# A sorted block attention with a gated feed-forward layer: a new order of the opening stage (value chunks behind key chunks, a four-fold mixing matrix, first weight loads behind the keys)

## The chip, the cores and the metric

The kernel runs on one core of one Trainium2 chip. The metric is the device time of one execution in microseconds (us), as the median of the runs. Names used: PE is TensorE (matmuls), PEld its weight loads, DVE is VectorE, ACT is ScalarE, POOL is GpSimd, SP is SyncE. SBUF is the working memory, PSUM the memory of eight banks into which PE writes; a bank has 512 float32 columns.

## The reference

```python
# q, k, v: (4 batches, 8 heads, 768 rows, 64); sort_net: (4, 8, 8, 8)
P = sort_net
for _ in range(5):                       # Sinkhorn: rows, then columns
    P = exp(P - max(P, -1)); P /= sum(P, -1) + 1e-9; P /= sum(P, -2) + 1e-9
# 8 blocks of 96 rows; each block of keys and values becomes a mix of all 8
k_sorted = einsum('bhij,bhjcd->bhicd', P, k_blocks)
v_sorted = einsum('bhij,bhjcd->bhicd', P, v_blocks)
attn = softmax(q_block @ k_sorted_block.T / sqrt(64))       # 96 x 96, per block
x = (attn @ v_sorted_block)  -> (3072 tokens, 512)
g = x @ w_gate               # 512 x 1536
out = (g * sigmoid(g) * (x @ w_val)) @ w_out                # 1536 x 512
```

All inputs and the output are float32; the kernel computes in bfloat16 with float32 sums.

## The kernel before

**Stages.** The 3072 tokens are eight groups of 384 (a half of the blocks of one batch, `n` = 0 to 7). For each group the attention gives `xts[(b, half)]`, four slices of 128 rows by 384 tokens; then `ffn(n)` makes 12 gate groups and 12 value groups of four matmuls each (`gate` L381, `value` L399), and three output tiles in three parts (`outp` L413), which run in the list of the next group. `merge` (L569) puts a list of side tasks (mixing of later batches' keys and values, scores, attention) between the gate and value groups, each task behind the point where the summed cost of the main list (0.65 for a gate or value group, 0.87 for a part of an output tile) reaches its due time. The order on PE and POOL is the program's. On DVE and ACT it is the program's up to L537 as well; from there on it is planned at compile time.

**The mixing.** The five Sinkhorn rounds work on `p_ps` (32 x 64, L193 to L211). Their result goes as `p_bf` (L186, L212 to L216) into `weights` (L461), where PE transposes it for every block i into `w_ps`: one matmul spreads one block over 64 partitions, eight copies of the 8 values of j, and `weights` runs once for the lower and once for the upper half. `mix_rows` (L467) multiplies `w_ps` by a 0/1 mask, which gives the block-diagonal mixing matrix `rmix` of a batch; that of batch 0 is made at once, those of batches 1 to 3 later (L490).

**The first 25 us** prepare batch 0 without any other work to lie beside. Its queue order is written out by hand:

- POOL issues all casting loads: v of batch 0 in two halves (L144, L145), half of q, k in two halves (L149), then copies its share of v into `vch` (`copy_v`, L150 to L152: each partition's 96 x 64 values turned round, so that one column is one d over all 96 rows c), then issues the first 256 columns of both weight matrices (`load_gv`, L153), the rest of q, three more `load_gv`, v of batch 1, the last two `load_gv`, and k, q of batch 1 and the output weights. At most eight such loads are under way; the ninth issue waits for the landing of the first.
- ACT copies the other share of v (L201, L203, L217, L218).
- PE keeps busy with small matmuls and fillers (`dots`, `fill`, L444 to L457), makes `w_ps`, and then chunks: `q0_chunk` (L249), `v_chunk` (L268) and `k0_chunk` (L258) each mix or transpose some columns into a PSUM tile, and DVE ("v") or ACT ("s") drains it to `kqt` or `vt`. The last argument is the PSUM tag: "a" and "b" are pairs of banks, "x" is one bank, "gen" is a set of three single banks, of which `w_ps` holds one until the last `mix_rows` has read it. A chunk waits for the drain of the one before it in its bank.
- `qk` (L323) makes the scores of one pair of heads over four blocks and their exponentials on ACT (`exps`); `av` (L326) multiplies them with `vt`, whose row carries 64 values and a one (so the 65th column is the sum), and DVE divides (`r_sb` L338, `st` L340). `x_to` transposes `st` into x, `drain` copies it, and `early` (L514) starts the first gate and value groups.

**Values of batch 1** are turned by POOL once they have landed (L595) and mixed by `v_chunk` inside `merge(ffn(1), ...)` (L608), followed by the keys and queries (`kqs`) and the first attention units of batch 1.

Of the kernel before, what the change touches and what calls it, by code (L numbers as in the profile page):

```python
# [10 lines left out]
BF16 = mybir.dt.bfloat16  # L11
AF = mybir.ActivationFunctionType
ALU = mybir.AluOpType
# [4 lines left out]
def kernel(  # L18
# [11 lines left out]
    nc = tc.nc  # L30

    B, H, S, D = q.shape
# [80 lines left out]
    def load_gv(lo, hi):  # L113
        load_w(wg_sb, wg_dram, lo, hi)
        load_w(wv_sb, wv_dram, lo, hi)

    def copy_v(eng, pair, rows, s, n=4, d0=0, d1=D):
        cs = slice(s * (C // n), (s + 1) * (C // n))
        dst = vch3[rows, d0:d1, cs]
        src = v_tiles[pair][rows, cs, d0:d1]  # L120
        if eng is nc.scalar:
            eng.copy(dst, src.transpose([0, 2, 1]))  # L122
        else:
            eng.tensor_copy(dst, src.transpose([0, 2, 1]))  # L124
# [22 lines left out]
    load_q0(0)  # L147
    for a, rows in enumerate(halves):
        nc.gpsimd.dma_start(out=k0[rows], in_=k_nat[0, :, a * HC:(a + 1) * HC, :])  # L149
    copy_v(nc.gpsimd, 0, lowr, 0)  # L150
    copy_v(nc.gpsimd, 0, lowr, 3)
    copy_v(nc.gpsimd, 0, lowr, 5, 8, 40, D)  # L152
    load_gv(0, 256)  # L153
    load_q0(1)
    for m in range(256, 1024, 256):
        load_gv(m, m + 256)
    load_v(1, 0, C)
    for m in range(1024, DF, 256):
        load_gv(m, m + 256)
    load_k(1, 0, C)  # L160
    load_q(1, 0, C)
    nc.gpsimd.dma_start(out=wo_sb, in_=wo_dram)
# [6 lines left out]

    def vt_tile(pair):  # L170
        if pair not in vts:
            t = vtp.tile([C, 2, H * NB, D + 4], BF16, name=f"vt{pair}", tag="vt")
            nc.vector.memset(t[:, :, :, D:D + 1].rearrange("p u n e -> p (u n) e"), 1.0)
            vts[pair] = t
        return vts[pair]
# [7 lines left out]

    rowreds = [const.tile([BH, NB, 1], FP32, name=f"rowred{it}") for it in range(N_ITER)]
    colred = const.tile([BH, 1, NB], FP32)
    p_bf = const.tile([BH, NB, H, NB], BF16)  # L186
    def pair_tile(name, tag):
        return psum.tile([128, 1024], FP32, name=name, tag=tag)

    def bank_tile(name, tag="gen"):  # L190
        return psum.tile([128, 512], FP32, name=name, tag=tag, bufs=3 if tag == "gen" else 1)

    p_ps = bank_tile("p_ps")[0:BH, 0:NB * NB].rearrange("p (i j) -> p i j", j=NB)  # L193
    for it in range(N_ITER):
# [14 lines left out]
        nc.vector.reciprocal(colred, colred)  # L209
        if it < N_ITER - 1:  # L210
            nc.vector.tensor_mul(p_ps, p_ps, colred.to_broadcast([BH, NB, NB]))  # L211
    for lo in (0, NB // 2):  # L212
        part = slice(lo, lo + NB // 2)
        nc.vector.tensor_tensor(
            p_bf[:, part], p_ps[:, part].unsqueeze(2).to_broadcast([BH, NB // 2, H, NB]),
            colred.unsqueeze(1).to_broadcast([BH, NB // 2, H, NB]), op=ALU.mult)  # L216
    copy_v(nc.scalar, 0, lowr, 4, 8)  # L217
    copy_v(nc.scalar, 0, lowr, 5, 8, 0, 40)  # L218

# [29 lines left out]
    def q0_chunk(t, at, n, eng, tag):  # L249
        dst = kqt_tile(0)[:, GI * C:2 * GI * C].rearrange("p (g t r c) -> p t g r c", g=H2, t=2, c=QC)[:, t]  # L250
        tp = chunk_tile("tq0", n // 8, tag).rearrange("p (l g r) -> p l g r", l=n, g=H2)
        for lc in range(n):
            for two in range(2):
                nc.tensor.matmul(tp[two * D:(two + 1) * D, lc], lhsT=q0[t][:, at + lc, :],
                                 rhs=sel[:, two], start=True, stop=True)
        drain(eng, dst[:, :, :, at:at + n], tp.rearrange("p l g r -> p g r l"))

    def k0_chunk(at, n, eng, tag):  # L258
        dst = kqt_tile(0)[:, 0:GI * C].rearrange("p (n a c) -> p a n c", a=2, c=HC)
        rm = rmix[0].rearrange("p a (g two) i -> p two a g i", two=2)  # L260
        tp = chunk_tile("tk0", n // 8, tag).rearrange("p (l a n) -> p l a n", l=n, a=2)
        for lc in range(n):
            for two in range(2):
                nc.tensor.matmul(tp[two * D:(two + 1) * D, lc].rearrange("p a (g i) -> p a g i", g=H2),
                                 lhsT=k0[:, at + lc, :], rhs=rm[:, two], start=True, stop=True)
        drain(eng, dst[:, :, :, at:at + n], tp.rearrange("p l a n -> p a n l"))

    def v_chunk(b, at, n, eng, tag):  # L268
        rows = slice(0, 128) if b % 2 else lowr
        dst = vt_tile(b // 2)[:, b % 2]  # L270
        mix = rmix[b][rows, 0].rearrange("p a b -> p (a b)")
        tp = chunk_tile("tv", n // 8, tag).rearrange("p (l n) -> p l n", n=H * NB)
        for ld in range(n):
            col = (at + ld) * C
            nc.tensor.matmul(tp[:, ld, :], lhsT=vch[rows, col:col + 128], rhs=mix,  # L275
                             start=True, stop=True)
        drain(eng, dst[:, :, at:at + n], tp[0:C].transpose([0, 2, 1]))
# [45 lines left out]
    def qk(b, u, tag="b"):  # L323
        exps(b, u, *scores(b, u, tag))

    def av(b, u, tag="a"):  # L326
        half, g = divmod(u, H2)
        vt = vts[b // 2][:, b % 2].rearrange("p (h i) e -> p h i e", h=H)
        av_ps = pair_tile("av_ps", tag).rearrange("p (two n) -> p two n", two=2)
        o = av_ps.rearrange("p two (i e) -> p two i e", i=4)  # L330
        for two in range(2):
            e = es[(b, u)][two]
            for i4 in range(4):
                nc.tensor.matmul(o[:, two, i4, 0:D + 1], lhsT=e[:, i4 * C:i4 * C + 128],  # L334
                                 rhs=vt[:, 2 * g + two, half * 4 + i4, 0:D + 1],
                                 start=True, stop=True)
        r_sb = ssp.tile([C, 2, 4, 1], FP32, name="r_sb", tag="r")
        nc.vector.reciprocal(r_sb, o[0:C, :, :, D:D + 1])  # L338
        st = ssp.tile([C, 4, 2, D], BF16, name="st", tag="st")
        nc.vector.tensor_tensor(st.rearrange("p i two d -> p two i d"), o[0:C, :, :, 0:D],  # L340
                                r_sb.to_broadcast([C, 2, 4, D]), op=ALU.mult)
        sts[(b, u)] = st
# [101 lines left out]
    def fill(tile, n):  # L444
        for _ in range(n):
            nc.tensor.matmul(tile, lhsT=warm_sb[:, 0:128], rhs=warm_sb, start=True, stop=True)  # L446
# [9 lines left out]
                         start=True, stop=True)  # L456
        fill(idle_ps, n)  # L457

    w_ps = bank_tile("w_ps")[:, 0:NB * B * H].rearrange("p (i b h) -> p i b h", b=B, h=H)

    def weights(half):  # L461
        for i in range(NB):
            nc.tensor.matmul(w_ps[halves[half], i].rearrange("p b h -> p (b h)"),
                             lhsT=p_bf[:, i].rearrange("p a b -> p (a b)"),
                             rhs=ident[0:BH, 0:BH], start=True, stop=True)

# [1 line left out]
        nc.vector.tensor_tensor(dst, mask[rows].unsqueeze(2).to_broadcast([R, H, NB]),  # L468
                                w_ps[rows, :, b].transpose([0, 2, 1]), op=ALU.mult)

    weights(0)
    weights(1)
    mix_rows(rmix[0][lowr, 0], lowr, 0)
    mix_rows(rmix[0][highr, 1], highr, 0)
    q0_chunk(0, 0, 16, "s", "b")
    v_chunk(0, 0, 8, "v", "gen")
    v_chunk(0, 8, 8, "s", "gen")
    v_chunk(0, 16, 16, "v", "a")
    v_chunk(0, 32, 8, "v", "gen")
    v_chunk(0, 40, 16, "s", "b")  # L480
    v_chunk(0, 56, 8, "s", "gen")
    k0_chunk(0, 16, "v", "a")
    k0_chunk(16, 16, "s", "b")
    k0_chunk(32, 8, "v", "gen")
    k0_chunk(40, 8, "s", "gen")
    q0_chunk(0, 16, 8, "v", "a")
    fill(idle_ps, 4)
    qk(0, 0, "a")
    qk(0, 1, "b")
    for b in range(1, B):  # L490
        rows = halves[b % 2]
        mix_rows(rmix["p"][rows, b % 2] if b > 1 else rmix[1][rows, 0], rows, b)
    qk(0, 2, "gen")
    idle_ps = bank_tile("idle_ps")
    fill(idle_ps, 2)
    av(0, 0, "a")
    fill(idle_ps, 2)
    av(0, 1, "b")
    fill(idle_ps, 1)
    xts[(0, 0)] = xtp.tile([128, H2, TW], BF16, name="xt0_0", tag="xt")  # L500
    qk(0, 3, "gen")
    av(0, 2, "a")
# [1 line left out]
    x_to(x01[:, 0], 0, 0)  # L504
    x_to(x01[:, 1], 0, 1)
    drain("s", xts[(0, 0)][:, 0:2, :], x01.rearrange("p g a b -> p g (a b)"))
    fill(idle_ps, 1)
    av(0, 3, "b")
    x2 = xt_tile("gen", 1)
    x_to(x2[:, 0], 0, 2)  # L510
# [47 lines left out]
    def kqs(b, ats):  # L558
        return [(at, lambda n=n: (kq_chunk(b, n * 32, 16, "v", "b"), kq_chunk(b, n * 32 + 16, 16, "s", "a")))
                for n, at in enumerate(ats)]  # L560

    def vs(f, size, ats):
        return [(at, lambda m=m: f(1, m * size, size, "sv"[m % 2], "ba"[m % 2])) for m, at in enumerate(ats)]
# [5 lines left out]
    def merge(main, side):  # L569
        done, k = 0.0, 0  # L570
        side = sorted(side, key=lambda t: t[0])
        for c, f in main:
            f()
            done += c
            while k < len(side) and side[k][0] <= done:
                side[k][1]()
                k += 1
        while k < len(side):
            side[k][1]()
            k += 1  # L580
# [22 lines left out]
    def q0_rest():  # L603
# [1 line left out]
        q0_chunk(1, 16, 8, "v", "a")  # L605

    merge(ffn(0), [(0.0, q0_rest)] + units(0, range(4, 8), (2.0, 6.6)))
    merge(ffn(1), vs(v_chunk, 16, (3.2, 3.9, 4.7, 5.5)) + kqs(1, (6.2, 8.2, 10.3))  # L608
          + units(1, range(4), (11.3, 16.4), (3.1, 2.5)))
    for s in range(4):  # L610
        copy_v(nc.gpsimd, 1, both, s)
# [43 lines left out]
```

## Time and profile before

| what | us |
|---|---|
| median of 3 runs | 248.45 (248.39 to 252.37) |
| the profiled execution | 249.62 |
| its span, first to last instruction | 247.7 |
| PE busy | 239.4 (97%) |
| PEld busy | 140.7 (57%) |
| DVE busy | 157.1 (63%) |
| ACT busy | 109.5 (44%) |
| POOL busy | 51.9 (21%) |
| granted TensorE clock | 1.000 |

Times of single events below are those of the profiled execution, counted from the start of its span. A busy engine is not an engine that sets the end: matmuls overlap, and PE's fillers count as busy. A line of the chain of work that ended last is a start, a length, and the engine with what it writes and the line of the code. In other rows the bracket gives the idle time of the engine just before, and what ended it.

### The profile page before, as it was taken

The page shows a single profiled execution, that of the slowest core. Times are in us where ns is not written, and L with a number is a line of the kernel's source. Part 1 is how long each engine was busy: PE and PEld are TensorE (multiplying, and loading weights), DVE is VectorE, ACT ScalarE, POOL GpSimd, SP SyncE. Part 2 cuts the span into 40 slices and gives each one's busy share as a digit, 9 for nine tenths or more (in the row PEclk, how much of TensorE's full clock was granted, in tenths as well). Part 3 has the DMA queues.
Part 4 walks back from the last instruction along what each step waited for, and adds up shares of the span by engine and source line. Part 5 has one row for each costly group of instructions (what it writes and reads, how often), then busy time and mean ns, then how long its engine had stood idle before and what let it go on. Part 6 is the DMA issues. An engine that isn't in the chain of part 4 may idle for free.

```text
span 247.7 us, 6185 instructions
## 1 busy us (share of the span) xinstructions
PE 239.4 (97%) x2633; PEld 140.7 (57%) x2633; DVE 157.1 (63%) x332; ACT 109.5 (44%) x186; POOL 51.9 (21%) x45
## 2 busy tenths in 40 slices
PE   8799998999999999999999999999999999999995
PEld 6375665666555556655555655565555555555543
DVE  6686789787556775857657646755764585446700
ACT  3877652453544444444642552354245334232311
POOL 5993459960049300000000000000000000000000
PEclk9999999999999999999999999999999999999999
DMA  5999999999999287010122121112111121100122
GB/s 98 214 120 181 218 191 219 194 227 215 215 164 179 41 201 173 4 42 3 45 56 52 55 62 34 44 42 78 32 42 45 39 57 54 42 21 25 42 81 88
DMA packets 39578, 24.38 MB, mean 98 GB/s; under 512 B 27712, under 2 KB 35648, under 8 KB 39104
## 3 DMA queue, kind: packets, MB, share of 16 engines
q0 software_dynamic: 21376, 14.16, 39.3%
q1 hardware_dynamic: 18176, 9.84, 13.9%
q8 instruction: 20, 0.33, 0.5%
q14 instruction: 6, 0.05, 0.1%
HBM read 28.32 MB, written 7.86 MB: 146 GB/s over the span
## 4 chain that ended last, share of the span: by engine, by line
PE 83%; DVE 9%; ACT 2%; issue 2%; DMA 2%; DVEq 0%; POOLq 0%
PE v_ps L403 23%; PE o_ps L420 23%; PE g_ps L385 22%; PE tkq L244 3%; PE av_ps L334 2%; PE qk L307 2%; DVE st L340 2%; DMA v<-in_v_dram 2%; DVE gs_sb L395 2%; DVE h L408 2%; DVE vt L222 1%; PE o_ps L436 1%; PE idle_ps L446 1%; PE tv L275 1%; ACT th_sb L393 1%
## 5 line engine op out<-in xcount | busy, mean ns | idle before, releaser
L395 DVE SCALAR_TENSOR_TENSOR gs_sb<-th_sb,g_ps 128x384 bf16<-128x384 bf16 x96 | 52.8, 550 | 51.5 <-ACT th_sb L393 48.7
L403 PE MATMUL v_ps<-xt,wv_sb 128*128 128x384 bf16 x380 | 77.3, 326 | 1.1 <-DVE st L340 0.7
L385 PE MATMUL g_ps<-xt,wg_sb 128*128 128x384 bf16 x376 | 76.7, 326 | 0.1
L393 ACT ACTIVATE th_sb<-g_ps 128x384 bf16<-128x384 f32 x96 | 47.1, 490 | 57.0 <-PE g_ps L385 54.5
L420 PE MATMUL o_ps<-wo_sb,h 128*128 128x512 bf16 x276 | 64.0, 379 | 0.0
L408 DVE SCALAR_TENSOR_TENSOR h<-v_ps,gs_sb 128x384 bf16<-128x384 f32 x96 | 53.3, 555 | 6.9
L403 PEld LDWEIGHTS <-wv_sb 128*128 128x128 bf16 x380 | 35.1, 97 | 24.9 <-issue 1.9
L385 PEld LDWEIGHTS <-wg_sb 128*128 128x128 bf16 x376 | 34.7, 97 | 23.5 <-issue 0.4
L420 PEld LDWEIGHTS <-h 128*128 128x128 bf16 x276 | 26.3, 98 | 28.9
L425 ACT COPY o_sb<-o_ps 128x512 f32<-128x512 f32 x23 | 13.5, 585 | 50.9 <-PE o_ps L420 50.9
L124 POOL COPY vch<-v 64x1536 bf16<-64x1536 bf16 (+2 forms) x11 | 28.6, 2635 | 21.1 <-DMA v<-in_v_dram 21.0
L320 ACT ACTIVATE e_all<-qk 96x768 bf16<-96x768 f32 x30 | 22.6, 802 | 7.6 <-PE qk L307 7.6
L340 DVE TENSOR_TENSOR st<-av_ps,r_sb 96x512 bf16<-96x512 f32 x32 | 21.7, 679 | 0.2
L334 PEld LDWEIGHTS <-e_all 96*128 96x128 bf16 x256 | 12.0, 97 | 4.9 <-ACT e_all L320 0.9
L334 PE MATMUL av_ps<-vt,e_all 96*128 96x65 bf16 x256 | 13.2, 193 | 0.0
L222 DVE CAST vt<-tv 96x1024 bf16<-96x1024 f32 (+1 forms) x9 | 9.8, 1096 | 2.6 <-PE tv L285 1.6
L338 DVE RECIPROCAL r_sb<-av_ps 96x8 f32<-96x8 f32 x32 | 6.4, 199 | 8.0 <-PE av_ps L334 7.9
L224 ACT CAST vt<-tv 96x1024 bf16<-96x1024 f32 (+1 forms) x9 | 8.1, 913 | 3.0 <-PE tv L285 1.8
L446 PE MATMUL idle_ps<-warm_sb 128*128 128x512 bf16 x25 | 7.7, 416 | 0.0
L222 DVE COPY oh_sb<-o_ps 128x256 f32<-128x256 f32 x1 | 0.4, 423 | 9.3 <-PE o_ps L436 9.3
L122 ACT COPY vch<-v 64x768 bf16<-64x768 bf16 (+1 forms) x4 | 5.4, 1375 | 0.7 <-DMA v<-in_v_dram 0.7
L370 POOL DMA_DIRECT2D q_scr<-in_q_dram x2 | 5.7, 3228 | 0.0
(80 smaller groups left out, 135.3 us busy)
## 6 DMA issues: line engine op xcount, KB each, us to landing
out_dram<-o_sb SPq DMA_DIRECT2D x23, 256.0 KB, 2.0
v<-in_v_dram POOLq DMA_DIRECT2D x3, 768.0 KB, 19.9
wg_sb<-in_moe_w_gate_dram POOLq DMA_DIRECT2D x6, 256.0 KB, 11.1
wv_sb<-in_moe_w_val_dram POOLq DMA_DIRECT2D x6, 256.0 KB, 11.9
wo_sb<-in_moe_w_out_dram POOLq DMA_DIRECT2D x1, 1536.0 KB, 23.8
kp<-in_k_dram POOLq DMA_DIRECT2D x2, 768.0 KB, 15.1
q_scr<-in_q_dram POOLq DMA_DIRECT2D x2, 768.0 KB, 29.9
v<-in_v_dram POOLq DMA_DIRECT2D x2, 384.0 KB, 6.4
```

Source lines behind the costliest of these rows:

```text
L124: eng.tensor_copy(dst, src.transpose([0, 2, 1]))
L222: nc.vector.tensor_copy(dst, src)
L320: nc.scalar.activation(e_all[:, n:n + 2, 0:4 * C], wide[0:C, :, 0:4 * C], AF.Exp, scale=scale)
L334: nc.tensor.matmul(o[:, two, i4, 0:D + 1], lhsT=e[:, i4 * C:i4 * C + 128], rhs=vt[:, 2 * g + two, half * 4 + i4, 0:D + 1], start=True, sto ...
L340: nc.vector.tensor_tensor(st.rearrange("p i two d -> p two i d"), o[0:C, :, :, 0:D], r_sb.to_broadcast([C, 2, 4, D]), op=ALU.mult)
L385: nc.tensor.matmul(g_ps, lhsT=wg_sb[:, kc, ts(m, 128)], rhs=xt[:, kc, :], start=(kc == 0), stop=(kc == NKC - 1))
L393: nc.scalar.activation(th_sb, g_ps, AF.Tanh, scale=0.5)
L395: nc.vector.scalar_tensor_tensor(gs_sb, th_sb, 1.0, g_ps, op0=ALU.add, op1=ALU.mult)
L403: nc.tensor.matmul(v_ps, lhsT=wv_sb[:, kc, ts(m, 128)], rhs=xt[:, kc, :], start=(kc == 0), stop=(kc == NKC - 1))
L408: nc.vector.scalar_tensor_tensor(h_tiles[n][:, m, :], v_ps, 0.5, gs_tiles.pop(m), op0=ALU.mult, op1=ALU.mult)
L420: nc.tensor.matmul(o_ps, lhsT=h_w[:, m, ts(t3, 128)], rhs=wo_sb[:, m, :], start=(m == 0), stop=(m == NFC - 1))
L425: nc.scalar.copy(o_sb, o_ps)
```

## The change

It reorders the first 25 us and two later places:

1. The first weight load (256 columns of both matrices) is issued behind k and ahead of POOL's copies of v.
2. The weight loads up to column 1280 go ahead of v of batch 1 (before: up to 1024).
3. A row of `vt` is 72 elements wide, not 68 (65 are used).
4. `p_bf` holds four copies of a block's row, not eight, written by one DVE instruction instead of two; `w_ps` is made by 32 matmuls over 32 partitions each instead of 16 over 64.
5. The chunks of batch 0 are cut and ordered anew: q's second chunk comes before the third value chunk, the last 16 of the 64 value columns come behind the keys, the keys are cut into 8, 8, 8, 16, 8, and the bank "x" is used for three chunks.
6. The four fillers ahead of the scores are half as wide and write into the unused half of the bank of `w_ps` (`fill_w`); the third scores come ahead of the mixing matrices of batches 1 to 3; there are fewer fillers behind.
7. The value chunks of batch 1 get later due times, and its key and query chunks too.

```diff
     for a, rows in enumerate(halves):
         nc.gpsimd.dma_start(out=k0[rows], in_=k_nat[0, :, a * HC:(a + 1) * HC, :])
+    load_gv(0, 256)
     copy_v(nc.gpsimd, 0, lowr, 0)
     copy_v(nc.gpsimd, 0, lowr, 3)
     copy_v(nc.gpsimd, 0, lowr, 5, 8, 40, D)
-    load_gv(0, 256)
     load_q0(1)
-    for m in range(256, 1024, 256):
+    for m in range(256, 1280, 256):
         load_gv(m, m + 256)
     load_v(1, 0, C)
-    for m in range(1024, DF, 256):
-        load_gv(m, m + 256)
+    load_gv(1280, DF)
...
-            t = vtp.tile([C, 2, H * NB, D + 4], BF16, name=f"vt{pair}", tag="vt")
+            t = vtp.tile([C, 2, H * NB, D + 8], BF16, name=f"vt{pair}", tag="vt")
...
-    p_bf = const.tile([BH, NB, H, NB], BF16)
+    p_bf = const.tile([BH, NB, 4, NB], BF16)
...
-    for lo in (0, NB // 2):
-        part = slice(lo, lo + NB // 2)
-        nc.vector.tensor_tensor(
-            p_bf[:, part], p_ps[:, part].unsqueeze(2).to_broadcast([BH, NB // 2, H, NB]),
-            colred.unsqueeze(1).to_broadcast([BH, NB // 2, H, NB]), op=ALU.mult)
+    nc.vector.tensor_tensor(p_bf, p_ps.unsqueeze(2).to_broadcast([BH, NB, 4, NB]),
+                            colred.unsqueeze(1).to_broadcast([BH, NB, 4, NB]), op=ALU.mult)
...
-    w_ps = bank_tile("w_ps")[:, 0:NB * B * H].rearrange("p (i b h) -> p i b h", b=B, h=H)
-
-    def weights(half):
-        for i in range(NB):
-            nc.tensor.matmul(w_ps[halves[half], i].rearrange("p b h -> p (b h)"),
+    w_bank = bank_tile("w_ps")
+    w_ps = w_bank[:, 0:NB * B * H].rearrange("p (i b h) -> p i b h", b=B, h=H)
+    for i in range(NB):
+        for lo in range(0, 128, 32):
+            nc.tensor.matmul(w_ps[lo:lo + 32, i].rearrange("p b h -> p (b h)"),
                              lhsT=p_bf[:, i].rearrange("p a b -> p (a b)"),
                              rhs=ident[0:BH, 0:BH], start=True, stop=True)
...
-    weights(0)
-    weights(1)
     mix_rows(rmix[0][lowr, 0], lowr, 0)
     mix_rows(rmix[0][highr, 1], highr, 0)
     q0_chunk(0, 0, 16, "s", "b")
-    v_chunk(0, 0, 8, "v", "gen")
-    v_chunk(0, 8, 8, "s", "gen")
-    v_chunk(0, 16, 16, "v", "a")
-    v_chunk(0, 32, 8, "v", "gen")
-    v_chunk(0, 40, 16, "s", "b")
-    v_chunk(0, 56, 8, "s", "gen")
-    k0_chunk(0, 16, "v", "a")
-    k0_chunk(16, 16, "s", "b")
-    k0_chunk(32, 8, "v", "gen")
-    k0_chunk(40, 8, "s", "gen")
-    q0_chunk(0, 16, 8, "v", "a")
-    fill(idle_ps, 4)
+    v_chunk(0, 0, 16, "v", "a")
+    v_chunk(0, 16, 8, "s", "gen")
+    v_chunk(0, 24, 8, "v", "gen")
+    q0_chunk(0, 16, 8, "s", "x")
+    v_chunk(0, 32, 16, "s", "b")
+    k0_chunk(0, 8, "v", "gen")
+    k0_chunk(8, 8, "s", "gen")
+    k0_chunk(16, 8, "v", "x")
+    k0_chunk(24, 16, "s", "a")
+    k0_chunk(40, 8, "v", "gen")
+    v_chunk(0, 48, 8, "v", "gen")
+    v_chunk(0, 56, 8, "v", "x")
+
+    def fill_w(n):
+        for _ in range(n):
+            nc.tensor.matmul(w_bank[:, 256:512], lhsT=warm_sb[:, 0:128], rhs=warm_sb[:, 0:256], start=True, stop=True)
+
+    fill_w(4)
     qk(0, 0, "a")
     qk(0, 1, "b")
+    fill_w(1)
+    qk(0, 2, "gen")
     for b in range(1, B):
         rows = halves[b % 2]
         mix_rows(rmix["p"][rows, b % 2] if b > 1 else rmix[1][rows, 0], rows, b)
-    qk(0, 2, "gen")
-    idle_ps = bank_tile("idle_ps")
+    av(0, 0, "a")
+    idle_ps = bank_tile("idle_ps", "x")
+    fill(idle_ps, 1)
+    av(0, 1, "b")
     fill(idle_ps, 2)
-    av(0, 0, "a")
-    fill(idle_ps, 2)
-    av(0, 1, "b")
-    fill(idle_ps, 1)
...
-    fill(idle_ps, 1)
     av(0, 3, "b")
...
-    merge(ffn(1), vs(v_chunk, 16, (3.2, 3.9, 4.7, 5.5)) + kqs(1, (6.2, 8.2, 10.3))
+    merge(ffn(1), vs(v_chunk, 16, (4.5, 5.2, 5.9, 6.6)) + kqs(1, (7.3, 8.9, 10.5))
           + units(1, range(4), (11.3, 16.4), (3.1, 2.5)))
```

## The prediction

> **What bounds the kernel now.** I read the table of 40 slices first (the clock granted to TensorE is 9 tenths or more in every slice, PE is at 9 or more nearly everywhere after slice 4), then the chain of work that ended last: PE has 83% of it, and after 25 us it is almost one unbroken row of matmuls. So a gain can only come from where PE waits: the first 25 us, or a hole later. The chain by itself from 10 to 21 us:
>
> ```profile
> 10.53 0.97 PE idle_ps L446 x4
> 11.50 0.00 issue
> 11.51 0.29 PE w_ps L463 x4
> 11.80 0.04 issue
> 11.84 0.43 PE w_ps L463 x12
> 12.27 0.62 PE tq L254 x32
> 12.90 0.35 PE tv L275 x8
> 13.25 0.02 issue
> 13.27 0.69 DVE vt L222
> ...
> 13.97 1.23 DVE vt L222
> ...
> 15.98 1.23 DVE kqt L222
> ...
> 17.70 0.97 PE idle_ps L446 x4
> 18.67 0.62 PE qk L307 x24
> ...
> 20.54 0.69 DVE st L340
> ```
>
> Columns: start, length, what. Between 13.27 and 18.4 the ends are set by drains on DVE and ACT and by the bank pairs they free (v, k0 and q0 chunks all pass through "a"); the scores start at 18.60 (the timeline's row; 18.67 here).
>
> The second view is the waits between 20 and 248 us. One alone names a transfer on PE's side; in the timeline it is
>
> ```profile
> 41.99 0.44 PEld L403 LDWEIGHTS <-wv_sb 128*128 128x128 bf16 x4 [0.84 <-DMA wv_sb<-in_moe_w_val_dram]
> 42.00 0.82 PE L403 MATMUL v_ps<-xt,wv_sb 128*128 128x384 bf16 x4 [0.70 <-DVE st L340]
> ```
>
> PE is idle 0.70 us. The matmul row names DVE, but the weight load says what it was: the last quarter-million bytes of the value weights, issued at 26.90, with 15.1 us to landing, so at 42.0. Third, the DMA view in stretches (us; PE, PEld, DVE, ACT, POOL busy; clock; DMA share; GB/s):
>
> ```profile
> 12.50:13.00 0.50, 0.50 (x32) 0.46 (x25) 0.24 (x2) 0.06 (x1) 0.50 (x2) 1.00 0.33 62
> 13.00:13.50 0.50, 0.50 (x23) 0.50 (x20) 0.23 (x1) 0.50 (x1) 0.50 (x1) 1.00 0.13 25
> 13.50:14.00 0.50, 0.43 (x15) 0.34 (x12) 0.49 (x2) 0.50 (x2) 0.50 (x2) 1.00 0.06 12
> 14.00:14.50 0.50, 0.49 (x17) 0.49 (x17) 0.50 (x1) 0.43 (x1) 0.50 (x2) 1.00 0.72 55
> 14.50:15.00 0.50, 0.50 (x21) 0.48 (x17) 0.50 (x1) 0.09 (x1) 0.50 (x2) 1.00 0.36 39
> ```
>
> The transfers run near 210 GB/s before 12.5 and near 190 after 15.5; between lies a hole, since POOL issues nothing from 4.60 to 12.85 (it waits for v, then copies).
>
> **Part 1: first weights issued behind keys.** Two issues of 0.78 us move from 12.85 to 4.60; they end at 6.16, and POOL's first copy waits for v until 6.51 (start 6.57) anyway. Cover 0.35 us; without it all three copies slip by what is missing, and the values with them (they end at 12.91, first used near 13). Behind the copies the other load of q, and every later load, is issued 1.55 us earlier. Gain in bytes: from 12.5 to 15.5 the six half-microsecond stretches (the five shown, and 160 GB/s in the next) moved 0.18 MB; at 190 they would have moved 0.57, so 0.39 MB / 190 GB/s = 2.0 us. I take 1.8 for every later landing; bounds 0 (the bytes only change places) and 2.0. The load at issue is late at 42.0 against 41.30, when PE is free; with 1.8 it lands at 40.2. So the 0.70 us go, if PE does not come more than 1.1 us earlier. What would be late next there: the bank that this value group takes was released by DVE's gs_sb at 40.73, so not that; the final x transposes' drain (xt) that the next gate group waits for at 44.86 hangs on the same PE work and moves with it. **-0.70** (0 to -0.75).
>
> **Part 2: batch 1's values later.** They now lie behind two more weight loads. All three together landed at 37.6 before, so with 1.8 gained v is in at 35.8 at the latest, against 34.97 now. POOL's four copies take 11.17, end 47.0. The value chunks of batch 1 stand two items later in the list (0.65 us each; behind the fourth gate group, not the third), at about 48.0 in the new time. Slack 1.0, cost 0; with no gain in part 1 they would be ready at 48.8 and cost up to 0.5. POOL's later issues (keys and values of batches 2, 3, the q casts) slip by 0.9, behind a queue that is full with wo until 54. The key chunks behind keep their distances (only the second moves one item towards the third, 1.73 us of output matmuls lie between): 0.
>
> **Part 3: four-fold matrix.** One DVE operation of 32x256 (0.40) in place of two: p_bf is whole at 11.43, not 11.78. PE is in its fillers until 11.50, so this saves only the 0.04 and the slower start. 32 weight matmuls of 32 columns replace 16 of 64. No row shows such a pair; the small matmuls of the start (L450) come at 3.49/124 = 28 ns, the 64-column ones at 0.43/12 = 36. So 0.90 to 1.15; I take 28 (the same 32 columns): end at 12.41 against 12.27, **+0.14** (to +0.39).
>
> **Part 4: the new order.** Rows used: DVE 1.23 for two banks, 0.69 for one; ACT 1.01 and 0.58; the next may start 0.09 before; tq 16 matmuls in 0.31, tv 16 in 0.48, tk 16 in 0.32. Of "gen" two banks are free while w_ps lives.
> q0 PE to 13.04, ACT 13.08 to 14.09. v 0-15 PE to 13.52, DVE 13.56 to 14.79. v 16-23 PE to 13.77, ACT 13.99 to 14.57. v 24-31 PE to 14.01, DVE 14.70 to 15.39. q0's rest PE to 14.33, ACT 14.49 to 15.07. v 32-47 ("b" free at 14.09) PE to 14.81, ACT 14.99 to 16.00. k 0-7 PE 14.81 to 15.13, DVE to 16.00. k 8-15 (bank at 15.39) PE to 15.75, ACT to 16.48. k 16-23 PE to 16.07, DVE to 16.78. k 24-39 PE to 16.71, ACT to 17.74. k 40-47 PE to 17.03, DVE to 17.74. v 48-55 DVE to 18.35, v 56-63 to 18.96.
> So q and k are whole at 17.74 where they were at 18.42; PE has four half-width fillers (0.12 each) until 18.0, and scores start at 18.02: 0.58 earlier. The moved values have a cover: exp (0.81, from 18.40 to 19.21) lies beside DVE's 1.22 for them; e is ready at 19.21, values at 18.96. Without that cover, 0.61 per drain. The mixing rows of batches 1 to 3 (0.68 on DVE) now stand ahead of the first reciprocal: 18.88 to 19.56, and av ends at 19.69. Slack 0.13. So the first st is 0.59 earlier, at 19.95. From there part comes back: the two fillers ahead of the fourth scores end at 20.7, its third av follows at 21.16 against 21.56, and the last st is at 22.80 against 23.21: **-0.40 for the whole front, with part 3 in it**. Bounds: -0.6 if DVE sets the pace alone, 0 if a slack of 0.13 to 0.35 breaks twice.
> Third scores ahead of the mixing: its two banks are free at 17.74 and 18.35, PE comes at 18.5; 0.
>
> **Part 5: rows of 72, fewer fillers.** Drains into kqt (stride 96 elements) and vt (68) take the same 1.23 and 1.01, so the stride's price is 0 on both sides. Fillers on PE fall from ten of 0.24 to three and five half ones, all in waits; the clock was 1.00 even in the stretch 8 to 10 us, where PE was busy 1.17 of 2.00, so 0.
> The Trainium skill speaks against this part: its page "TensorE: Matmul & The Clock Gate", section "Part 1: The HAM clock gate", says that a mostly idle window of some 3.4 us halves the clock. This trace shows no halving anywhere. By that rule, were it met at 19 us, one window at half speed would add an estimated 1.7 us, and the sum would be +0.6. In my schedule no gap of PE is longer than 0.6 us.
>
> **Sum.** -0.40 - 0.70 = -1.1. The profiled execution took 249.62 for a span of 247.70 (1.92 around it): span 246.6, execution 248.5. The runs' median, 248.45, lies 1.17 under the profiled one; it falls to 247.35. Beyond the hand-ordered front the order on DVE and ACT is planned anew; PE's waits for DVE after 60 us are 0.4 and 0.2, so I add 0.5 either way: 246.7 to 248.0.
>
> **Rivals.** (1) The hole at 42 only changes its name. DVE is without a pause from 39.5 to 42.7 us; if the planner puts an st ahead of the gate's gs_sb (0.55 + 0.68), the bank is late and PE waits as long as before. For it: the profile's 0.70 names DVE. Against: the weight load names the DMA, and the bank was out at 40.73. Then only the front is left: 248.05.
> (2) Slower: the weights issued at 4.60 share the 16 engines with keys that have not landed. k's second half lands at 4.07 + 10.4 = 14.47, the first k chunk now wants it at 14.81. For it: landings of neighbours overlap in this trace (768 KB of v came 2.7 us after 256 KB that were just ahead). Against: they land in the order of issue. If they share evenly, k is late by up to two weight loads, 2.6 us by the spacing of landings at 25.3, 26.6 and 27.9: k at 17.1, its 96 matmuls (1.92) to 19.0, the last drain to 19.7, scores at 19.75, 1.15 later than before. Less the 0.70 at 42: +0.45, 248.9; with v's second half late too, 249.5. It is slower from a k landing at about 16.65 on.
> (3) It does more: with the last filler and stall gone the gate group at 44 loses its wait of 0.3 as well, and a hole of 0.5 near 64 to 70 closes in the new plan: 246.5.
> (4) It does not do what it says: the copies hold the values anyway and the 32 small matmuls take 1.15, so the front gains 0; the 0.70 stays gained: 247.75, inside the forecast's own range.
>
> **How the numbers follow.** Forecast with (4) 0.58, (1) 0.15, (2) 0.14, (3) 0.07, an accident I have not seen, beyond 249.5, 0.06. The range 246.5 to 249.2 leaves out the half of (3), the accident and the dear end of (2). 2% of 248.45 is 5.0 us, about what a measurement of this kernel can tell from no change. No named case comes near it; two thirds of the accident lie beyond it: faster 0.01, same 0.95, slower 0.04.
>
> **What would show it.** Right: transfers without a hole from 12 to 15 us; scores at 18.0 and the first st at 19.95; no wait on wv_sb near 41; batch 1's first value chunk without a wait for POOL. Wrong: tk waiting for a transfer near 15; PE idle at 41 with DVE as releaser; clock under 1.00 near 20; a vt drain behind 19.3.

## The result, and the profile after

The changed kernel took 251.12 us (median of 6 runs, 250.30 to 252.44); the kernel before, run beside it, 248.49. The ratio is 1.0109 with an interval from 1.0076 to 1.0142: slower by about 1.1%. (Ratios leave out runs of either kernel that lie over 1.5% above its fastest; medians and ranges of runs hold them.) The profiled execution is the longest of the six: 252.44, span 250.5, granted clock 0.986 (before: 249.62, 247.7, 1.000).

The chain of work that ended last, after, for the stretch that was shown of before (start, length, what):

```profile
14.63 1.40 PE tk L260 x75
16.03 1.90 issue
17.92 0.51 PE tk L260 x21
18.43 0.96 PE tv L271 x16
19.39 0.97 PE w_ps L485 x4
20.36 0.75 PE qk L303 x9
```

In the middle of the keys' 96 matmuls, after 75 of them, PE stands still for 1.9 us and waits for nothing that the profile names. Before and behind the pause the same line runs on. The rows behind it are slow too: the four half-width fillers (`fill_w`, L485 in this trace) take 0.97, booked at 0.48; the value chunk's 16 matmuls 0.96, booked at 0.48. The stretches say why (us; PE, PEld, DVE, ACT, POOL busy; clock; DMA share; GB/s):

```profile
14.00:16.00 2.00, 1.78 (x90) 1.63 (x87) 1.75 (x4) 1.98 (x3) 2.00 (x4) 1.00 1.42 209
16.00:18.00 2.00, 0.10 (x7) 0.08 (x6) 0.40 (x1) 0.00 (x0) 2.00 (x4) 1.00 1.14 197
18.00:20.00 2.00, 2.00 (x41) 1.63 (x40) 1.53 (x3) 1.01 (x1) 1.27 (x2) 0.59 1.43 198
20.00:22.00 2.00, 2.00 (x31) 1.20 (x30) 0.85 (x4) 1.16 (x2) 0.66 (x2) 0.50 1.48 200
...
24.00:26.00 2.00, 1.83 (x33) 1.49 (x32) 1.05 (x3) 1.27 (x3) 0.62 (x2) 0.71 1.45 196
```

PE is busy 0.10 of 2.00 from 16 to 18 us, ACT not at all, and the granted clock then falls to a half until some way into the stretch from 24. The page's table of 40 slices has the same as one digit, in the slice from 18.8 to 25.0:

```profile
PEclk9995999999999999999999999999999999999999
```

The transfers ran as part 1 wanted. The hole of 12.5 to 15 us, where before moved 62, 25 and 12 GB/s in the first three half microseconds, is filled:

```profile
12.50:13.00 0.50, 0.50 (x22) 0.50 (x21) 0.00 (x0) 0.50 (x1) 0.50 (x2) 1.00 0.84 144
13.00:13.50 0.50, 0.50 (x23) 0.45 (x21) 0.45 (x1) 0.47 (x2) 0.50 (x2) 1.00 1.28 177
13.50:14.00 0.50, 0.50 (x24) 0.46 (x25) 0.50 (x1) 0.47 (x2) 0.50 (x1) 1.00 1.44 201
```

And the wait at 42 us is gone; the value group in its place follows the matmuls ahead of it without idle time (its row in the timeline has no bracket):

```profile
40.84 0.33 PE L347 MATMUL x_ps<-ident,st 96*128 96x96 bf16 x4
41.01 0.82 PE L399 MATMUL v_ps<-xt,wv_sb 128*128 128x384 bf16 x4
```

**Where the time went.** The first gate group (in `early`) starts at 26.44 after and at 23.36 before: +3.08. The span grew by 2.8, so behind the front 0.28 came back. Two single waits make up 0.32 of that: -0.70 for the wait at 42, and +0.38 for a second pause of the same kind, in a key chunk of batch 1:

```profile
63.25 0.66 PE L240 MATMUL tkq<-rmix,kq 128*64 128x64 bf16 x30 [0.38 <-issue]
```

**What the pause waits for.** The page of after lists a queue that the prediction never looked at:

```profile
q8 instruction: 20, 0.33, 0.5%
```

Twenty packets of some 16 KB (0.33 MB / 20), moved by the engines that move the data. In half-microsecond stretches of the DMA view, the second of them ran in before between 14.0 and 14.5 us, in the hole of the transfers:

```profile
q8 instruction: 1, 0.02, 12.0%
```

In after no such packet runs between 14.0 and 15.5; it comes between 15.5 and 16.0:

```profile
q8 instruction: 1, 0.02, 12.2%
```

Narrower stretches of the same view place the start at 14.23 in before and at 15.68 in after; PE goes on at 17.92, 2.2 us after it. The second pause is the same: a packet starts at 61.03, and PE goes on at 63.25. The theory to be tested: PE's instructions arrive in these packets, and with the hole filled the next one comes too late. Its rivals: a piece of data (k or v) is late, the new order of the front is itself bad, or the later dates of batch 1's chunks cost the time.

The Trainium skill, page "Runtime: NRT & Kernel Launch", section "Instruction fetch mechanics", states that an engine's instructions are refilled in 16 KiB blocks of 256, and that crossing a block is mostly hidden. By that figure PE's 5,271 recorded instructions are an estimated 20.6 blocks, where the profile counts 20 packets; that it is mostly hidden holds for most of them in this trace and not for two, of which one cost 1.9 us and one 0.38.

### The profile page after: what moved, and what is told of

The parts are those of the page before. It is cut to its first block, busy times and chain, and to the rows that moved or that the text cites. A ratio compares the mean times of both kernels' runs of the same rounds, so it can differ in the third digit from the quotient of the medians.

```text
span 250.5 us, 6192 instructions
## 1 busy us (share of the span) xinstructions
PE 238.1 (95%) x2624; PEld 141.8 (57%) x2647; DVE 156.8 (63%) x332; ACT 109.8 (44%) x186; POOL 52.0 (21%) x45
## 4 chain that ended last, share of the span: by engine, by line
PE 82%; DVE 6%; DMA 5%; issue 4%; ACT 2%; POOL 1%; DVEq 0%; POOLq 0%
PE v_ps L399 23%; PE g_ps L381 22%; PE o_ps L416 21%; PE av_ps L330 3%; DMA v<-in_v_dram 3%; PE tkq L240 3%; PE qk L303 3%; DVE gs_sb L391 2%; DMA xt<-st 2%; PE tv L271 2%; DVE h L404 1%; DVE st L336 1%; POOL vch L124 1%; PE o_ps L432 1%; PE tk L260 1%
## 5 line engine op out<-in xcount | busy, mean ns | idle before, releaser
L416 PE MATMUL o_ps<-wo_sb,h 128*128 128x512 bf16 x255 | 61.5, 379 | 1.3 <-issue 0.3
L330 PEld LDWEIGHTS <-e_all 96*128 96x128 bf16 x256 | 12.5, 100 | 4.3 <-issue 0.2
L218 DVE CAST vt<-tv 96x1024 bf16<-96x1024 f32 (+1 forms) x10 | 10.4, 1054 | 3.0 <-PE tv L281 1.6
L303 PEld LDWEIGHTS <-kqt 64*128 64x128 bf16 x128 | 3.5, 102 | 4.2 <-issue 1.7
L303 PE MATMUL qk<-kqt 64*128 64x96 bf16 x128 | 5.1, 222 | 0.6 <-DVE st L336 0.4
```

The lines of the kernel that those rows point to most:

```text
L303: nc.tensor.matmul(pss[two][:, i4 * C:(i4 + 1) * C], lhsT=k_sb[lo:lo + D, k_at + at:k_at + at + 128], rhs=q_sb[lo:lo + D, q_at + at:q_at + ...
L416: nc.tensor.matmul(o_ps, lhsT=h_w[:, m, ts(t3, 128)], rhs=wo_sb[:, m, :], start=(m == 0), stop=(m == NFC - 1))
```

## The experiments

Each kernel was timed beside the kernel before. Medians of before were 248.57 (first four kernels), 248.59 (next four) and 248.54 (last four). The remarks behind # in the edits are this document's.

### The early load taken back (e1_late_weights)

```diff
-    load_gv(0, 256)            # behind k
     copy_v(nc.gpsimd, 0, lowr, 0)
...
+    load_gv(0, 256)            # behind the copies, as before
```

> The changed kernel with the first weight load back behind POOL's copies; everything else stays. Theory A (PE's next block of code is fetched over the same 16 transfer engines; the early weight load fills the hole between 12.5 and 15 us in which that fetch went out at 14.2 before, so it goes out at 15.8 and PE, out of code, stands still from 16.0 to 17.9): the fetch goes out by 14.5, no gap of PE over 0.3 us between 12 and 18 us, scores start at 17.5 to 18.2, the clock stays at 1.00. The hole at 42 is back, since the last value weights land at 42.0 again and PE comes earlier (wait 1.0 to 1.4). Time 248.0 to 249.2, as before the change. Rival B (the pause belongs to the new order on PE itself, 32 weight matmuls and short key chunks, and not to the transfers): the gap of 1.9 us stays in the fourth key chunk, clock drops again, 250 to 252. Rival C (keys land late because the weights share the engines): as A here.

Median 250.05 (248.46 to 252.35, 10 runs), ratio 1.0024 (0.9990 to 1.0058); profiled 250.26, span 248.2, clock 1.00. The pause is gone: scores start at 17.52, where they start at 20.30 after, and the first gate group at 22.27. So the new order alone is early, and the early load makes the pause: without it the packet starts at 13.44. The time was missed (248.0 to 249.2 were expected), since not all of the gain is kept. PE waits 0.65 for value weights at 40.2, 0.78 at 60.4 (the second pause, whose packet starts at 58.74) and, since v of batch 1 now landed at 37.5,

```profile
48.72 0.47 PE L271 MATMUL tv<-rmix,vch 128*128 128x64 bf16 x10 [0.71 <-POOL vch L124]
```

### The early load alone (e2_early_only)

```diff
+    load_gv(0, 256)            # in the kernel before, behind k
     copy_v(nc.gpsimd, 0, lowr, 0)
...
-    load_gv(0, 256)
```

> The kernel before, with the first weight load issued ahead of POOL's copies and nothing else changed. Theory A: the code fetch that went out at 14.2 goes out at 16 or later; PE reaches the end of its code in the last q chunk (11 of its 16 matmuls, near 17.5) and stands there for 1 to 2 us; scores start near 20 instead of 18.6; the wait for the value weights at 42 is gone; 249 to 251.5, with the clock lowered in some runs. Rival B: no gap, only the gain at 42: 247.7 to 248.0. Rival C: PE waits ahead of the first key chunk, near 15.3, for the transfer of k, 1 to 2 us.

Median 249.69 (249.42 to 250.39, 10 runs), ratio 1.0027 (0.9996 to 1.0057), clock 1.00 in all ten. The old order has a pause as well, at the end of its keys (chain of work):

```profile
15.67 1.11 PE tk L264 x59
16.78 1.16 issue
17.95 0.26 PE tk L264 x5
```

It was expected in the last q chunk and came five key matmuls ahead of it. The packet starts at 15.58, much as in after, and PE goes on 2.4 later; the pause is shorter because PE reaches its place later in the old order, at 16.78 and not 16.03. The wait at 42 is gone. So the load makes a pause under either order, and a pause of 1.16 did not lower the clock in any of the ten runs. The time is in the expected range.

### The same code moved by 48 matmuls (e3_dots172)

```diff
-    dots(124)
+    dots(172)
```

> The changed kernel with 172 small filler matmuls at its start in place of 124: 96 more instructions (load and matmul each) on PE, executed while PE has nothing else to do, so that every later matmul lies 96 instructions further on in PE's code and blocks of code end 48 matmuls earlier in the work. Theory A: the gap of PE moves by 48 matmuls: it comes after about 26 of the 96 key matmuls (in the second key chunk, near 15.3) and no longer after 75; 1 to 2.5 us long; time within 1 us of the changed kernel. Rival B and rival C: the gap stays where it is, after 75 key matmuls in the fourth chunk, at 16.0.

Median 253.21 (253.06 to 255.25, 4 runs), ratio 1.0180 (1.0104 to 1.0257); clock 0.980 to 0.993. The 48 more small matmuls lie in PE's idle start. The timeline of PE:

```profile
14.48 0.83 PE L260 MATMUL tk<-rmix,qk 128*64 128x64 bf16 x27
17.75 1.58 PE L260 MATMUL tk<-rmix,qk 128*64 128x64 bf16 x69 [2.44 <-issue]
```

After, the pause came behind 75 key matmuls; with 48 more matmuls ahead it comes behind 27, which is 75 - 48. Neither a bank, nor a drain, nor a transfer of data goes by the number of matmuls executed since the start: this is a place in PE's code, and the packet ran later than 15 us here too (15.32, PE goes on 2.4 later). The stretch from the start of the span to the start of the pause counts the same for after, e2_early_only and this kernel, in that order: 349 matmuls (the first x) and 351 weight loads (the second), though the three differ in order or in length ahead of it.

```profile
0.00:16.03 16.03, 12.21 (x349) 8.90 (x351) 10.77 (x45) 11.51 (x16) 14.33 (x21) 1.00 0.93 163
0.00:16.78 16.78, 13.02 (x349) 9.66 (x351) 11.95 (x46) 11.23 (x16) 15.53 (x23) 1.00 0.94 166
0.00:15.31 15.31, 12.68 (x349) 9.41 (x351) 10.13 (x44) 10.78 (x15) 13.63 (x20) 1.00 0.91 160
```

The kernels below with a pause in the keys (e4, e7, f1, f4) count the same.

The time was missed: within 1 us of the changed kernel was expected, and the median is 2.1 above. The profile shows a longer pause (2.44 for 1.90) and a longer second one (1.16 at 60.3, for 0.38), and all four runs have a lowered clock, where three of the six of after do not. The half clock lasts less long here, 3.4 us (0.61 in the stretch from 18 to 20, 0.54 from 20 to 22, then 1.00).

### Half of the early load (e4_half_early)

```diff
-    load_gv(0, 256)            # behind k
+    load_w(wg_sb, wg_dram, 0, 256)
     copy_v(nc.gpsimd, 0, lowr, 0)
...
+    load_w(wv_sb, wv_dram, 0, 256)
```

> The changed kernel with only the gate half of the first weight load (256 KB) ahead of POOL's copies and the value half behind them. Theory A: about half of the hole is left; the fetch goes out between 14.2 and 15.0, PE's gap falls to 0 to 0.9 us, the clock stays at 1.00 if the gap is under about 1 us, and the wait at 42 is gone or under 0.3, as the later loads still come earlier: 247.2 to 248.8. Rival B: the gap of 1.9 stays, 250 to 252. Rival C: half of the delay of the keys, a gap of about 1 us ahead of the first key chunk.

Median 249.01 (248.42 to 249.78, 10 runs), ratio 1.0005 (0.9973 to 1.0036), clock 1.00. The packet starts at 13.96, and PE pauses from 15.81 to 16.46 (0.65), behind the same 75 matmuls. The pause goes with the bytes that stand in the queue: 0 for none, 0.65 for 256 KB, 1.90 for 512 KB. The median lies 0.2 above the expected 247.2 to 248.8, the profiled execution (248.47) inside.

### The kernel before once more (e5_before_again)

No edit.

> The kernel before, unchanged, for a second trace: the first one is 1.1 us longer in its span (247.7) than most other runs of this kernel (246.5). If the hole of 0.70 us at 42 (value weights landing late) is a habit of the kernel, it is here again with 0.5 to 0.9 us in a span near 246.5. If it belongs to that one slow execution, PE has no gap over 0.2 us between 38 and 45 us, and the gain that the prediction booked there never existed for the median.

One execution: 248.54, span 246.6. In the stretch from 40 to 42 us PE is busy throughout, where the first profile of before had it at 1.28 (this execution, then the first):

```profile
40.00:42.00 2.00, 2.00 (x15) 1.22 (x15) 2.00 (x5) 0.49 (x1) 2.00 (x2) 1.00 1.00 209
40.00:42.00 2.00, 1.28 (x11) 0.65 (x9) 2.00 (x6) 0.49 (x1) 2.00 (x2) 1.00 1.08 216
```

This execution has no wait for weights at 42; v also landed 0.35 earlier (6.16, not 6.51). Both together, 0.70 + 0.35, make up the 1.1 us by which the two executions differ. The wait that part 1 was to remove belonged to a longer execution of before, not to its median.

### The new front alone, twice (e6_front_only, f3_front_again)

The changed kernel with the loads and batch 1's due times as before:

```diff
-    load_gv(0, 256)            # behind k
     copy_v(nc.gpsimd, 0, lowr, 0)
...
+    load_gv(0, 256)
     load_q0(1)
-    for m in range(256, 1280, 256):
+    for m in range(256, 1024, 256):
...
-    merge(ffn(1), vs(v_chunk, 16, (4.5, 5.2, 5.9, 6.6)) + kqs(1, (7.3, 8.9, 10.5))
+    merge(ffn(1), vs(v_chunk, 16, (3.2, 3.9, 4.7, 5.5)) + kqs(1, (6.2, 8.2, 10.3))
```

> The changed kernel with the order of all weight and value loads, and the due times of batch 1's mixing, as before; left are the four-fold matrix, the new order of chunks, the fillers and the rows of 72. Theory A (code fetches wait for transfers; the front's order by itself is a gain): no gap of PE over 0.3 us between 12 and 18, scores at 17.3 to 17.8 (18.6 before), clock 1.00, and neither the wait for POOL near 48 nor the gap near 60 in a key chunk, both seen with the new load order and due times; 247.4 to 248.2, or 248.3 to 248.7 if the wait for the value weights at 42 takes the gain back. Rival B (the front's order on PE is what costs): a gap of 0.5 us or more between 12 and 18 or near 60 stays, 249 to 251.

> The front's order alone once more, for a trace of one of its longer executions: of ten, four took 247.4 to 247.8 and the others 249.7 to 252.4. Theory A expects a longer one to have a gap of PE with its code arriving late (2.1 to 2.4 us after the fetch starts), at the end of a block, by chance of the transfers; no such gap in a short one. The rival: the longer ones wait for data (v, k or weights landing late) and have no gap in mid chunk.

First: median 249.85 over ten runs, in two clumps (four from 247.40 to 247.81, six from 249.66 to 252.43), ratio 0.9998 (0.9958 to 1.0038). The median misses the expected 247.4 to 248.7 and lies where rival B was put; the four short runs are inside. The profile is of a short one (247.44, span 245.5): no pause, scores at 17.42, first gate group at 22.18, the earliest time of a kernel seen so far. Second: median 249.25 (248.23 to 252.50, 8 runs), ratio 1.0022 (0.9985 to 1.0059), and the profile fell on a longer run (249.96, span 248.0). Its front is as early (gate group at 22.01), no pause for code is in it, and PE stands still later (timeline, PE and its weight load):

```profile
37.45 0.82 PE L400 MATMUL v_ps<-xt,wv_sb 128*128 128x384 bf16 x4 [0.71 <-DMA wv_sb<-in_moe_w_val_dram]
40.10 0.82 PE L382 MATMUL g_ps<-xt,wg_sb 128*128 128x384 bf16 x4 [0.28 <-DMA wg_sb<-in_moe_w_gate_dram]
42.30 0.44 PEld L400 LDWEIGHTS <-wv_sb 128*128 128x128 bf16 x4 [1.35 <-DMA wv_sb<-in_moe_w_val_dram]
```

The last of them leaves PE idle 1.21. Together 2.20 of the 2.5 us by which this execution is longer than the short one. So this long run waits for weights, not for code, as the rival in the expectation had it: PE comes over 1 us earlier (gate group at 22.01, not 23.36) to weights whose landing varies. The other long runs have no trace.

### Front and half of the early load (e7_front_half, f1_half_rows68)

```diff
+    load_w(wg_sb, wg_dram, 0, 256)      # e6_front_only, behind k
     copy_v(nc.gpsimd, 0, lowr, 0)
...
-    load_gv(0, 256)
+    load_w(wv_sb, wv_dram, 0, 256)
```

> The same, with the gate half of the first weight load ahead of POOL's copies. Theory A: the gap in the fourth key chunk is back with 0.4 to 0.9 us (PE's code arrives 2.1 to 2.4 us after the fetch starts near 14.0), but no gap near 60 and none at 42: 247.6 to 248.5, against the front alone better only if the wait at 42 was there. Rival B: as the front alone, 249 or more.

Median 248.06 (247.71 to 248.36, 10 runs), ratio 0.9965 (0.9944 to 0.9986): below the kernel before by 0.35%, as expected (247.6 to 248.5), and with hardly any scatter. A pause of 0.73 is left at 15.90; no wait at 42 or 60. Half of the early load buys the landings for 0.7 us of PE's code.

The same with rows of 68 (`D + 4`):

> The front with the gate half early (which ran at 247.7 to 248.4), with rows of 68 elements in place of 72. If the rows cost nothing, as the unchanged means of drains and matmuls say: 247.7 to 248.4 again, ratio 0.994 to 0.999. If rows of 72 cost the 0.6% that the run with rows alone seemed to show: 246.3 to 247.2.

Median 248.39 (248.06 to 248.85, 11 runs), ratio 0.9989 (0.9970 to 1.0008), at the upper edge of what was expected if the rows cost nothing (0.994 to 0.999). The pause is 0.53 here. The kernel with 68 is not faster than that with 72, so the rows do not hide a cost of 0.6% in it. As a near repeat of e7_front_half it also says that the gain of 0.35% is not firm: this interval holds 1.

### Rows of 72 alone, twice (e8_rows72, f2_rows72_again)

```diff
-            t = vtp.tile([C, 2, H * NB, D + 4], ...)     # in the kernel before
+            t = vtp.tile([C, 2, H * NB, D + 8], ...)
```

> The kernel before with rows of 72 elements in place of 68 in the mixed values, nothing else. The prediction's price of 0: ratio 0.997 to 1.003. If the wider stride cost or gained in the drains or in the attention matmuls, their mean times would move by more than 10 ns (before: 1.10 us a drain on DVE, 193 ns a matmul) and the ratio with them.

> Rows of 72 alone once more, in more rounds, since five runs scattered from 248.6 to 251.7 and the kernel before scatters too (most at 248.4 to 248.8, some up to 251). Cost 0: most runs at 248.4 to 248.8, ratio 0.998 to 1.003. A real cost: most runs above 249, ratio above 1.003.

250.01 over 5 runs, ratio 1.0060 (1.0016 to 1.0104), which misses the expected 0.997 to 1.003, and then 248.81 over 12, ratio 1.0026 (0.9999 to 1.0052), which meets it, six of these between 248.37 and 248.57, where most runs of before lie. The profiled executions of both wait for weights near 41 (0.42, and 0.40 + 0.94). The operations did not change: DVE's two-bank drain into `vt` is 1,215 ns and `av`'s matmul 193 ns, in before and in both runs. No operation shows a cost of the rows; that they lengthen the runs in another way, by up to 0.5% by the second interval and more by the first, is not excluded.

### The new front with the whole early load (f4_front_full)

```diff
+    load_gv(0, 256)            # e6_front_only, behind k
     copy_v(nc.gpsimd, 0, lowr, 0)
...
-    load_gv(0, 256)
```

> The front's order with the whole first weight load ahead of POOL's copies, the other loads and batch 1's due times as before the change: only the early load is added to the front alone. Theory A: fetch at 15.4 to 15.9, gap of 1.5 to 2.2 us in the fourth key chunk, the clock down in some runs, no gap near 60 and none at 42; 249.2 to 251.5, about 0.4 less than the changed kernel by the missing gap near 60. If the order of batch 1's values is a large part of the loss: under 249.

Median 251.44 (250.31 to 251.79, 4 runs), ratio 1.0102 (1.0068 to 1.0135), inside the expected 249.2 to 251.5; clock 0.986 in three, 0.993 in the fourth. The packet starts at 15.32. In the chain of work

```profile
15.91 1.78 issue
17.68 0.75 PE tk L261 x21
```

and from 18 us on a clock of 0.50. There is no pause near 60 here and no wait at 42. The early load on the new front gives the whole loss by itself; the order and the dates of batch 1's values and keys are not needed for it.

## Why the prediction was wrong, step by step

**Part 1 is the step that failed,** by its treatment of the hole. The words "between lies a hole" were read as 2.0 us of lost bandwidth. It was the time in which the second packet of code of the span came in. Filling it delayed that packet from 14.23 to 15.68 and stopped PE for 1.9 us. The step's lower bound, "the bytes only change places", left no room for a loss, because the list of queues was read as data only; the line of q8 stood in the page of before too.

**Its gain was mis-sized as well.** The -0.70 appeared in the traces as forecast, yet against the median it is nearly nothing: an execution of before at 248.54 has no such wait. "The runs' median, 248.45, lies 1.17 under the profiled one" was noted, and then the whole saving of the longer execution was taken from the median. What half of the early load does buy is less scatter: 247.71 to 248.36 in e7_front_half, 248.06 to 248.85 in f1_half_rows68, and without it (e6_front_only) 247.40 to 250.42 even if the two longest runs are left out.

**Part 5, the clock.** "In my schedule no gap of PE is longer than 0.6 us" fell with part 1, and a sign that the prediction named for being wrong, a clock under 1.00 near 20, came. The clock is the larger share of the loss in the profiled execution: its front is 4.26 later than in e6_front_only (26.44 against 22.18), 1.89 of it the pause, and the 2.4 left lie almost all in the stretch at half clock. Over the runs of after it comes and goes: three at 0.999 to 1.000 took 250.30 to 251.01, three at 0.986 to 0.991 took 251.24 to 252.44. It goes with the pause and not with the fewer fillers, which e1, e4, e6 and e7 have too, at 1.00 in all but one of their 40 runs (that one 0.979, as one of the 74 runs of before beside the experiments). The rule of the Trainium skill that the prediction set aside thus did bear on this change, though the pause was 1.9 us, shorter than its window. The rows of 72 show no price in any operation; a small one is left open above.

**Part 3 had the wrong sign.** The 32 small matmuls took 0.30 (11.20 to the next row's 11.50), not 0.90 to 1.15, against 0.69 for the 16 of before (11.51 to 12.20). The rows of before and after:

```profile
11.51 0.77 PE L463 MATMUL w_ps<-ident,p_bf 32*64 32x32 bf16 x16
11.20 0.37 PE L459 MATMUL w_ps<-ident,p_bf 32*32 32x32 bf16 x32
```

That is 9 ns each after; the 28 was taken from matmuls that each use the same part of the array. The four in a row here write to four different strips of 32 partitions. The Trainium skill has a reason that fits, page "TensorE: Matmul & The Clock Gate", section "Part 3: Packing small matmuls — row/col tiling": matmuls at different 32 x 32 places of the array run at the same time. No run here changes that alone. So -0.39 where +0.14 was booked.

**Part 4 was right and too low.** Scores were to start at 18.02 and do so at 17.42 in e6_front_only; 0.53 of the 0.60 between is what part 3 had wrong. The first gate group comes 1.18 earlier than in the profiled before, 0.81 earlier than in e5_before_again. The best runs follow: 247.40 against 248.38, -0.98 where -0.40 was booked; the medians of that order (249.85, 249.25) do not, and its one long run with a trace waits for weights.

**Part 2** cost nothing while the early load stood, and 0.71 without it (e1_late_weights). Its "The key chunks behind keep their distances" missed the 0.38 at 62.87. All four kernels with the new order of the later loads and the new dates pause there (0.38 in after, 0.78 in e1, 1.16 in e3, 0.22 in e4); f4_front_full, which has both as before, does not. Which of the two it is was not tried.

**The rivals.** Rival (2) had the right place, the right side and the right cause (transfers that share the engines) with the wrong victim: k's second half was at 14.57, 10.5 after its issue, as booked. Rival (1) did not happen. Rival (3), 246.5, was reached by no run; the lowest is 247.40. Rival (4) fell with e6_front_only.

**Open:** the trace shows when a packet of code runs, not when PE asked for it, so how far ahead a block is wanted is inferred from 2.2 to 2.5 us between packet and restart. That more bytes queued ahead make the packet late is shown by e1, e4 and f4, and by how far PE was when it started: behind 226 to 242 matmuls without the early load (before, e1, e5, e6, e8, f2, f3), 271 to 274 with half of it (e4, e7, f1) and 290 to 349 with all of it (after, e2, e3, f4). Which of the engines it waited for is not shown. And between a pause of 1.16, which left the clock alone, and one of 1.78, which lowered it, lies a bound that these runs do not place; nor do they show why three of the six runs of after kept their clock, or why the half clock lasted 3.4 us in e3 and 6.8 in after and f4.

## What to carry to other kernels

Before a hole in the transfers is filled, see what else runs in it: list the instruction packets in short stretches and ask which block of an engine's code comes in there, above all where that engine runs many short instructions. A wait seen in one profiled execution is a saving against the median only if that execution is a typical one; compare its time with the runs first, or profile twice. And an idle "issue" of over a microsecond in the middle of one loop of like matmuls is a hint of late code: add some instructions far ahead of it and see whether it moves by just as many.

## What the runs showed of the hardware

- PE can run out of code behind data transfers: pauses of 0.53 to 2.44 us in the keys, each ending 2.2 to 2.5 us after a 16 KB instruction packet had begun. The place follows the number of instructions (349 recorded matmuls from the start in all seven kernels with the pause; 75 into the keys, and 27 with 48 more ahead).
- Pauses of 1.90 and 1.78 us were followed by half the granted clock for about 6.8 us in the profiled executions of after and f4_front_full, one of 2.44 by 3.4 us of it (e3_dots172); 1.16 and less were not.
- Matmuls of 32 x 32 that go to four strips of partitions in turn took 9 ns each; 28 ns was the nearest row of before.
- The landing of the weights varies between executions of one kernel by enough to leave PE idle for 0 to 2.2 us; issuing a part of them earlier narrowed the runs from 3.0 us (e6_front_only without its two longest) to 0.65 (e7_front_half) and 0.79 (f1_half_rows68).
